# Sliding-window attention in 18 blocks with a DMA transpose of the output, instead of 17 blocks with a TensorE transpose

## The chip, the cores and the metric

The kernel runs on one NeuronCore of a Trainium2 chip. The core has TensorE (PE, matmuls), VectorE (DVE), ScalarE (ACT), GpSimd (POOL) and SyncE (SP), which here only issues DMAs. The metric is the device time of one execution in microseconds, lower is better. Several executions are timed, and one more is profiled.

## What is computed

A transformer layer with adaptive layer norm for 2048 tokens of 448 features. Attention has 16 heads of 28 features, and each token looks at 8 tokens: itself and every second one before it (dilation 2), so even tokens see only even tokens and odd ones only odd ones.

```python
mod = (silu(c) @ w_mod)                     # sa, ca, ga, sb, cb, gb
h = layernorm(x) * (1 + ca) + sa
qkv = h @ wqkv                              # 16 heads of 28
idx = pos[:, None] - (arange(8) * 2)[None, :]
logits = where(idx >= 0, q . k[idx] * 28 ** -0.5, -1e9)
o = softmax(logits) . v[idx]
x = x + ga * (o @ wo)
h = layernorm(x) * (1 + cb) + sb
x = x + gb * (gelu(layernorm(h) @ w1 + b1) @ w2 + b2)
```

## The kernel before

The tokens are stored as two halves: first the 1024 even ones, then the 1024 odd ones. In this order the window is the 8 nearest tokens of a half, and a block of queries needs a band of neighbouring keys. There are 16 stripes of 128 tokens.

**Front end.** For each group of stripes (0-1, 2-3, 4-7, 8-11, 12-15; the group's name is its first stripe) the input is normalized (`z`), transposed into feature-major form (`zt`: by TensorE for the first three groups, by DMA for the last two, L569), scaled (`h`, tile `hT`), and projected to keys and queries (`qk`, eight items a group, L599), which `qe` copies to `qT` and `kT`. These tiles have 16 columns of padding at both ends.

**Attention.** 17 blocks of 121 queries, each with 128 keys that begin 7 tokens before the first query (`attention`, L664). A block is a chain of items, and their names, followed by the block's number, are used throughout:
- `lt` (TensorE, L678): 16 matmuls, one a head, four at a time in row tiles of 32, give logits transposed (keys x queries) in four PSUM banks.
- `ex` (ScalarE, L689): four exponentials into the tile `et`, bfloat16.
- `mk` (VectorE, L696): `et` times a mask of zeros and ones that was expanded to all heads beforehand (`mask_rest`, L658); two blocks have small extra memsets, for the start of the sequence and the border of the halves.
- `pv` (TensorE, L711) and `ve`: the values of the 128 keys, straight from `hT`, and their copy to SBUF with a column of ones.
- `po` (TensorE, L721): weights times values for 16 heads; the column of ones gives the sum of the weights.
- `rd`, `on` (VectorE, L728 and L732): reciprocal of the sum, and the normalized output, tokens by 448 features.
- `pt` (TensorE, L742): four 128x128 transposes of `on` into PSUM. The last one starts at feature 320, so that no padding of `on` is needed; the output projection has zeros in the doubled rows.
- `ot` (ScalarE or VectorE, through `copy`): the transposed block goes to `oT`, which holds 1024 tokens, the second half over the first.

**Rest.** `wo` projects a stripe (L763), `x1` adds it to the input, and a second and third normalization (`s2`, `r2`, `z2`, `ml`, `ad`, `s3`, `r3`, `y`) give `y`, transposed by DMA (`yt`, L803) into `yT`. In chunks of four stripes the feed-forward part follows: `w1` and `wt` (L295 and L300), `ge` (ScalarE, L812), `w2` (L853), `fin` (VectorE, L866 and L868), and `out`, a store of the stripe (L872). The power in a normalization (`r2`, `r3`, `frs`) is computed by GpSimd (L469).

**Order.** All items are declared to a planner (`Plan`) with an estimated cost for each engine that may run them, what they need, and which buffers they take. `order()` sorts them by these costs and by constants (`PRI` for each kind, `NUDGE` for single items, `LOOK`, `PHASES` for how many attention blocks come before each chunk), picks the engine where there is a choice, and gives out the eight PSUM banks. The instructions are then issued in this order, so each engine, and SP with its DMAs, works through a fixed list and waits where an operand isn't ready. SP issues the loads, the transposes by DMA and the stores.

Of the kernel before, what the change touches and what calls it, by code (L numbers as in the profile page):

```python
# [17 lines left out]
KOFF_N = [0, 128, 256, 320]  # L18
ZR_N = 64
# [3 lines left out]
PADF = 16  # L23
BQ, BK = 121, 128
NBK = -(-S // BQ)
WT = PADF + S + PADF
# [5 lines left out]
PHASES = [9, 14, 17, 17]  # L32
# [11 lines left out]
LOOK = 0.000444  # L44

PRI = {"ad": -96.0, "agfst": 196.2, "ags2": 257.8, "ags3": 51.1, "ex": -118.3, "ge": -9.0, "h": 492.2,
       "lt": 26.7, "mk": -63.3, "ml": 15.5, "mod": -71.9, "on": -63.1, "ot": -130.2, "pb": -18.2, "po": 77.9,
       "ps": 105.4, "pt": 35.7, "pv": 19.9, "qe": -91.5, "qk": -123.7, "r3": 22.0, "rd": -24.1, "s2": -207.6,
       "s3": 72.9, "ve": -158.2, "w1": -18.3, "w2": -62.8, "wo": -144.0, "wt": 10.8, "x1": 20.5, "y": -37.1,
       "yt": -87.3, "z": 139.3, "z2": 81.0, "zt": -267.4}  # L50

NUDGE = {"ad10": -20.7, "ad6": -81.4, "ad8": 11.5, "ags2_0": 10.6, "ags2_11": -6.6, "ags2_14": -75.9,
       "ags2_2": -100.4, "ags2_5": -6.3, "ags2_8": -10.9, "ags3_11": -15.8, "ags3_14": 104.5, "ags3_3": 36.6,
       "ags3_5": -16.0, "ags3_7": -64.8, "ex11.2": 12.3, "fin9": -40.2, "frs12a": 19.8, "frs8a": 22.6,
       "ge2.10": 13.7, "ge2.8": 76.9, "ge3.12": 31.1, "h12.0": 37.1, "h4.2": 55.2, "h8.2": 78.5, "lt0": 93.2,
       "lt10": 29.5, "lt12": 5.8, "lt13": 52.0, "lt15": -33.2, "lt2": -20.6, "lt4": 58.9, "lt8": -8.9,
       "mk5": 34.4, "mk8": 47.0, "ml10": -42.6, "ml4": 10.8, "on12": -18.4, "on4": 8.5, "ot11": 74.0,
       "ot12": 9.8, "ot16": 53.8, "ot4": 60.9, "ot5": 22.7, "ot6": 65.9, "out13": -24.4, "out14": -59.4,
       "out8": -106.6, "pb_cbe": -184.9, "pb_gb": -36.7, "pb_gbe": -13.6, "po0": 8.9, "po1": -60.3, "po12": 10.8,
       "po15": -157.0, "pt10": 41.4, "pt12": 14.3, "pt5": -52.4, "pt8": -37.2, "pv1": -38.0, "pv13": -62.4,  # L60
       "pv4": 11.4, "pv7": 25.6, "qe12.0": -27.8, "qe12.3": 18.7, "qe12.5": 61.8, "qe2.0": -34.0, "qe2.1": 132.4,
       "qe2.2": 4.0, "qe2.3": 19.6, "qe2.4": 7.9, "qe2.6": 9.4, "qe2.7": -33.6, "qe4.0": 62.7, "qe4.7": -12.7,
       "qe8.0": 5.1, "qe8.1": -64.2, "qe8.7": -80.1, "qk0.1": 133.8, "qk12.0": 113.6, "qk12.6": 61.1,
       "qk4.1": -47.9, "qk4.3": 67.4, "qk4.4": 55.2, "qk4.5": -100.0, "qk4.7": 76.7, "qk8.7": -37.3,
       "r2_0": -89.0, "r2_0a": 57.1, "r2_10": 15.5, "r2_4": -9.3, "r2_6": -40.7, "r2_8": -62.2, "r3_0": 23.2,
       "r3_0a": 24.8, "r3_10a": -7.1, "r3_12": -88.9, "r3_12a": -80.6, "r3_6": 21.3, "r3_6a": -73.9, "r3_8": 9.0,
       "r3_8a": 38.0, "rd12": 24.6, "rd13": 26.1, "rd4": 14.1, "rd6": 54.8, "s2_11": 64.8, "s2_15": -82.0,
       "s2_5": -15.7, "s2_6": 35.8, "s2_8": 10.9, "s3_0": -51.5, "s3_1": 12.8, "s3_10": 26.8, "s3_11": 17.0,
       "s3_12": 28.7, "s3_13": -42.2, "s3_7": 38.2, "s3_9": -24.9, "w1_0.5": 32.1, "w1_1.6": 54.9, "w1_2.0": 6.1,
       "w1_2.2": -19.8, "w1_3.6": 57.3, "w2_11.1": 53.2, "w2_14.2": 103.0, "w2_14.3": 80.6, "w2_14.6": -16.7,  # L70
       "w2_15.2": -35.7, "w2_4.3": -44.4, "w2_5.6": 48.3, "w2_8.2": 135.9, "w2_9.2": 147.8, "w2_9.3": -21.2,
       "w2_9.4": -70.7, "w2_9.5": 107.8, "w2s2": 74.7, "wo0": 8.8, "wo1": 19.3, "wo11": -16.1, "wo8": 34.2,
       "wt_0.5": -16.3, "wt_2.3": -8.1, "wt_2.5": 20.1, "x1_1": 21.7, "x1_10": -25.3, "x1_11": -5.0,
       "x1_5": 27.9, "y11": -18.1, "y5": 40.1, "yt1": 28.5, "yt10": -133.2, "yt11": -10.4, "yt12": -68.4,
       "yt2": 6.1, "z1": 95.3, "z2": 138.5, "z2_10": 23.2, "z2_11": -10.3, "z2_12": -125.8, "z2_13": 16.8,
       "z2_2": 8.2, "z2_4": 21.3, "z2_5": 19.0, "z2_8": 41.6, "z2_9": 13.3, "z4": 6.2, "z8": 12.9, "zt13": -4.0,
       "zt4": 5.5, "zt8": 84.8}
# [162 lines left out]
def kernel(  # L240
# [65 lines left out]
    def ps_of(nm, n=512):  # L306
        return psum[P.bank[nm]][:, 0:n]

    hT = cst.tile([128, KT, WT], BF16, name="hT")
    qT = cst.tile([128, 4, WT], BF16, name="qT")  # L310
    kT = cst.tile([128, 4, WT], BF16, name="kT")
# [20 lines left out]
    mask1 = cst.tile([128, BK], BF16, name="mask1")  # L332
    mask_rest = cst.tile([128, H, BK], BF16, name="mask_rest")
# [4 lines left out]
    ybufs = [cst.tile([128, DP], BF16, name=f"ybuf{i}") for i in range(NYB)]  # L338
    NVB = 3
# [27 lines left out]
    load_ktiles(nc.sync, wo_s, A_wo, ZR_N)  # L367
# [22 lines left out]
    nc.vector.memset(wo_s[0:ZR_N, KT - 1, :], 0.0)  # L390
# [9 lines left out]
    pad_ranges = [(0, PADF), (PADF + S, WT)]  # L400
    for (a, b) in pad_ranges:
        nc.gpsimd.memset(hT[:, :, a:b], 0.0)
        nc.gpsimd.memset(kT[:, :, a:b], 0.0)
        nc.gpsimd.memset(qT[:, :, a:b], 0.0)
    nc.gpsimd.memset(mask1[:], 1.0)
    nc.gpsimd.affine_select(out=mask1[:], in_=mask1[:], pattern=[[1, BK]], compare_op=ALU.is_ge,
                            fill=0.0, base=WIN - 1, channel_multiplier=-1)
    nc.gpsimd.affine_select(out=mask1[:], in_=mask1[:], pattern=[[-1, BK]], compare_op=ALU.is_ge,
                            fill=0.0, base=0, channel_multiplier=1)

    def tok_col(b):
        return PADF + b * 128

# [197 lines left out]
    zs, h_of, fe_of = {}, {}, {}  # L611
# [39 lines left out]
    def b1_fn(e):  # L651
# [6 lines left out]
    P.add("mask", {"DVE": 0.65}, needs=["later"], fn=lambda e: nc.vector.tensor_copy(  # L658
        out=mask_rest[:], in_=mask1[:].unsqueeze(1).to_broadcast([128, H, BK])))

# [3 lines left out]
    def attention(g, exp_after, lt_after):  # L664
        q0 = PADF + g * BQ
        k0 = q0 - (WIN - 1)
        nq = min(BQ, S - g * BQ)
        fes = sorted({fe_of[min(max(t, 0), S - 1) // 128] for t in range(g * BQ - WIN + 1, g * BQ + BK)})
        fek = sorted({fe_of[min(max(t, 0), S - 1) // 128] for t in range(g * BQ - WIN + 1, g * BQ + BQ)})
# [4 lines left out]
        def l_fn(e):  # L674
            lts = T["lt", g] = [ps_of(f"lt{g}.{r}") for r in range(4)]
            for ft in range(4):
                for r in range(4):
                    nc.tensor.matmul(lts[r][:, ft * BK:(ft + 1) * BK],  # L678
                                     lhsT=kT[32 * r:32 * r + DH, ft, k0:k0 + BK],
                                     rhs=qT[32 * r:32 * r + DH, ft, q0:q0 + BK],  # L680
                                     start=True, stop=True, tile_position=(32 * r, 0))
        P.add(f"lt{g}", {"PE": 0.25}, rows=32, after=lt_after, needs=[f"qe{f}.{m}" for f in fes for m in range(8)], lag=0.17,
              allocs=[f"lt{g}.{r}" for r in range(4)] + [f"et{g}"], fn=l_fn)
        for r in range(4):
            def x_fn(e, r=r):
                if r == 0:
                    T["et", g] = wk.tile([128, H, BK], BF16, name="et", tag="et")
                et_v = T["et", g][:].rearrange("p (ft r) c -> p r ft c", r=4)
                nc.scalar.activation(out=et_v[:, r], in_=T["lt", g][r].rearrange("p (ft c) -> p ft c", ft=4),  # L689
                                     func=ACT.Exp, scale=float(DH) ** -0.5)  # L690
            P.add(f"ex{g}.{r}", {"ACT": 0.57}, needs=[f"lt{g}"], tab="exp",
                  after=exp_after + ([f"ex{g}.{r - 1}"] if r else []), uses=[f"lt{g}.{r}", f"et{g}"], fn=x_fn)

        def m_fn(e):
            et = T["et", g]
            nc.vector.tensor_tensor(out=et[:], in0=et[:], in1=mask_rest[:], op=ALU.mult)  # L696
            if g == 0:
                nc.vector.memset(et[0:WIN - 1, :, 0:WIN], 0.0)
            jx = SL - g * BQ
            if 0 < jx < BQ:  # L700

                px = jx + WIN - 1
                p0 = (px - (WIN - 1)) // 32 * 32
                assert px - 1 <= p0 + 31
                nc.vector.memset(et[p0:px, :, jx:jx + WIN], 0.0)
        P.add(f"mk{g}", {"DVE": 1.14}, needs=[f"ex{g}.{r}" for r in range(4)] + ["mask"], uses=[f"et{g}"], fn=m_fn)
# [11 lines left out]
        def o_fn(e):  # L718
            po = T["po", g] = ps_of(f"po{g}", H * (DH + 1)).rearrange("p (h d) -> p h d", h=H)
            for h in range(H):  # L720
                nc.tensor.matmul(po[:, h, :], lhsT=T["et", g][:, h, :], rhs=vbufs[g % NVB][:, h, :],  # L721
                                 start=True, stop=True)
# [212 lines left out]
```

## Time and profile before

| | |
|---|---|
| median of 3 runs | 182.32 us (181.95 to 182.45) |
| profiled execution | 182.19 us |
| its span, first to last instruction | 180.5 us |
| granted TensorE clock | 1.0 |
| HBM read, written | 9.41 MB, 1.84 MB |
| DMA traffic after the loads (from about 29 us) | short bursts: transposes and stores |

In rows of grouped instructions the columns are: line, engine, operation, output and inputs by the program's names, shapes and count; then the total busy time in microseconds and the mean duration of one in nanoseconds; then the engine's idle time before them and what ended it. `PEld` is TensorE's weight load, which overlaps its matmuls. In the chain that ended last, a row has a start, a length and what ran. A row of the waits names who waited, for whom, the total, the number of times and the longest. In the rows of DMA issues the last number is the median time from issue to landing.

### The profile page before, as it was taken

The numbers are of one execution on the slowest core, as the hardware profiler recorded it, in microseconds if no ns is written. First come the engines' busy times: TensorE is split into PE (matmuls) and PEld (weight loads), VectorE is DVE, ScalarE is ACT, GpSimd is POOL, SyncE is SP. The second block draws the span as 40 slices with busy tenths as digits, with TensorE's granted clock in tenths as the row PEclk, the third lists the DMA queues.
The fourth block names the chain that finished last, engine by engine and source line by source line (L and its number), as shares of the span: only waits on it lengthen the run. The fifth ranks groups of instructions, "written<-read, shape, count | busy, mean of one in ns | idle before, by whom it ended". The sixth has DMA issues, their size and how long they took to land.

```text
span 180.5 us, 3837 instructions
## 1 busy us (share of the span) xinstructions
PE 174.4 (97%) x1464; PEld 88.4 (49%) x1464; DVE 138.4 (77%) x348; ACT 118.6 (66%) x217; POOL 32.7 (18%) x67
## 2 busy tenths in 40 slices
PE   6989999999999999999999999999999999999992
PEld 2457566555555544444655454445643454433451
DVE  5789899799998999997989988688879865020251
ACT  2298996999898946999578475995835810077400
POOL 8413005000106403121403041100013400000000
PEclk9999999999999999999999999999999999999999
DMA  5999995441000530011051012031000025100011
GB/s 166 322 368 315 401 390 162 94 86 29 0 4 0 61 61 0 0 35 32 22 79 35 4 21 63 0 73 41 0 4 25 0 56 120 47 25 0 0 51 51
DMA packets 23376, 14.63 MB, mean 81 GB/s; under 512 B 13693, under 2 KB 22398, under 8 KB 23358
## 3 DMA queue, kind: packets, MB, share of 16 engines
q1 hardware_dynamic: 22334, 13.53, 27.0%
q10 hardware_dynamic: 1024, 0.86, 1.5%
q8 instruction: 11, 0.18, 0.4%
q14 instruction: 7, 0.06, 0.1%
HBM read 9.41 MB, written 1.84 MB: 62 GB/s over the span
## 4 chain that ended last, share of the span: by engine, by line
PE 72%; DVE 12%; DMA 4%; ACT 4%; SPq 2%; issue 2%; ACTq 1%; POOL 1%; DVEq 0%
PE ps L295 21%; PE ps L853 20%; PE ps L599 8%; PE ps L763 6%; PE ps L711 5%; PE ps L300 4%; DVE st L446 4%; DMA hT<-zbuf 3%; PE ps L721 3%; PE ps L678 2%; DVE et L696 2%; PE ps L742 2%; SPq L803 2%; DVE hT L589 2%; DMA yT<-ybuf 1%
## 5 line engine op out<-in xcount | busy, mean ns | idle before, releaser
L812 ACT ACTIVATE hm<-ps,b_col 128x512 bf16<-128x512 f32 x56 | 34.1, 692 | 23.2 <-PE ps L300 23.1
L853 PE MATMUL ps<-w_s,hm 128*128 128x448 bf16 x224 | 47.2, 353 | 0.0
L469 POOL TENSOR_TENSOR rs<-tv,neg_half 128x2 f32<-128x2 f32 (+1 forms) x21 | 20.4, 973 | 108.8 <-DVE ng L465 108.7
L295 PE MATMUL ps<-yT,w_s 128*128 128x512 bf16 x168 | 39.5, 380 | 0.5 <-DMA yT<-ybuf 0.5
L689 ACT ACTIVATE et<-ps 128x512 bf16<-128x512 f32 x68 | 36.1, 613 | 3.3 <-PE ps L678 3.0
L599 PE MATMUL ps<-hT,Wqk 128*128 128x512 bf16 (+1 forms) x160 | 31.3, 337 | 0.9 <-ACT Wqk L436 0.9
L853 PEld LDWEIGHTS <-hm 128*128 128x128 bf16 x224 | 21.0, 98 | 19.3 <-issue 0.9
L295 PEld LDWEIGHTS <-w_s 128*128 128x128 bf16 x168 | 15.5, 98 | 21.9 <-issue 5.3
L866 DVE TENSOR_TENSOR xt<-ps,gbb_bc 128x448 f32<-128x448 f32 x11 | 6.9, 624 | 22.3 <-PE ps L853 22.3
L696 DVE TENSOR_TENSOR et<-et,mask_rest 128x2048 bf16<-128x2048 bf16 x17 | 20.5, 1208 | 0.1
L599 PEld LDWEIGHTS <-Wqk 128*128 128x128 bf16 x160 | 14.6, 97 | 11.4 <-POOL nb L471 1.1
L446 DVE BATCH_NORM_STATS2 st<-x_all 128x6 f32<-128x448 bf16 x32 | 18.5, 613 | 0.1
L711 PE MATMUL ps<-Wv,hT 128*128 128x448 bf16 x68 | 15.7, 353 | 0.0
L763 PE MATMUL ps<-wo_s,oT 128*128 128x448 bf16 x64 | 14.1, 352 | 0.0
L768 DVE TENSOR_TENSOR x_all<-ps,x_all 128x448 bf16<-128x448 f32 x16 | 9.7, 619 | 3.1 <-PE ps L763 3.0
L436 ACT CAST vbuf<-ps 128x448 bf16<-128x448 f32 x14 | 7.6, 546 | 5.0 <-PE ps L711 5.0
L436 ACT CAST qT<-ps 128x512 bf16<-128x512 f32 (+1 forms) x19 | 9.6, 518 | 2.0 <-PE ps L599 1.5
L721 PEld LDWEIGHTS <-et 128*128 128x128 bf16 x272 | 9.0, 96 | 3.8 <-DVE et L696 0.9
L732 DVE TENSOR_TENSOR on<-ps,rden 128x448 bf16<-128x448 f32 x17 | 10.5, 616 | 0.2
L436 ACT CAST kT<-ps 128x512 bf16<-128x512 f32 (+1 forms) x18 | 8.9, 512 | 1.3 <-PE ps L599 1.1
L721 PE MATMUL ps<-vbuf,et 128*128 128x29 bf16 x272 | 9.5, 176 | 0.1
L446 DVE BATCH_NORM_STATS2 st<-z 128x6 f32<-128x448 bf16 x16 | 9.4, 612 | 0.1
(98 smaller groups left out, 188.7 us busy)
## 6 DMA issues: line engine op xcount, KB each, us to landing
w_s<-in_B_w_dram SPq DMA_DIRECT2D x2, 896.0 KB, 11.4
out_dram<-x_all SPq DMA_DIRECT2D x16, 112.0 KB, 1.7
w_s<-in_B_w_dram SPq DMA_DIRECT2D x1, 1568.0 KB, 13.7
wmod<-in_w_mod_dram SPq DMA_DIRECT2D x1, 1344.0 KB, 7.5
x_all<-in_A_x_dram SPq DMA_DIRECT2D x1, 896.0 KB, 10.4
wqk_st<-in_A_wqkv_dram SPq DMA_DIRECT2D x2, 336.0 KB, 5.8
x_all<-in_A_x_dram ACTq DMA_DIRECT2D x2, 224.0 KB, 4.2
x_all<-in_A_x_dram SPq DMA_DIRECT2D x1, 448.0 KB, 5.0
```

The costliest lines, as they stand in the source:

```text
L295: nc.tensor.matmul(o, lhsT=lhs(w, slice(0, 128), kt), rhs=rhs(slice(0, 128), kt), start=(i == 0), stop=False)
L436: nc.scalar.copy(out=out, in_=in_)
L446: nc.vector.bn_stats(out=st[:], in_=src())
L469: nc.gpsimd.tensor_tensor(out=rs[:], in0=T["tv", tile_key][:], in1=neg_half[:, 0:n], op=ALU.pow)
L599: nc.tensor.matmul(pq, lhsT=Wqk[:, kt, m, :], rhs=hT[:, kt, c0:c0 + w], start=(kt == 0), stop=(kt == KT - 1))
L689: nc.scalar.activation(out=et_v[:, r], in_=T["lt", g][r].rearrange("p (ft c) -> p ft c", ft=4), func=ACT.Exp, scale=float(DH) ** -0.5)
L696: nc.vector.tensor_tensor(out=et[:], in0=et[:], in1=mask_rest[:], op=ALU.mult)
L711: nc.tensor.matmul(pv, lhsT=hT[:, kt, k0:k0 + BK], rhs=Wv[:, kt, :], start=(kt == 0), stop=(kt == KT - 1))
L721: nc.tensor.matmul(po[:, h, :], lhsT=T["et", g][:, h, :], rhs=vbufs[g % NVB][:, h, :], start=True, stop=True)
L763: nc.tensor.matmul(pw, lhsT=oT[:, kt, jb * 128:(jb + 1) * 128], rhs=wo_s[:, kt, :], start=(kt == 0), stop=(kt == KT - 1))
L812: nc.scalar.activation(out=T["hm", c][:, ft, 0:w], in_=ps_of(f"p1_{c}.{ft}", w), func=ACT.Gelu_apprx_tanh, bias=b1_col[:, ft:ft + 1])
L853: nc.tensor.matmul(T["p2", b], lhsT=T["hm", c][:, ft, bi * 128:(bi + 1) * 128], rhs=w2_s[:, ft, :], start=(ft == 0 and b not in XPE), stop ...
```

## The change

Attention works in blocks that begin at multiples of 112 after a first block of 128 in each half: `BLOCKS` lists nine a half, 18 in all. A block of 112 queries has 128 keys, the first 16 of them before its first query; a block of 128 has exactly its own tokens as keys. So no block crosses the border of the halves, the padding of `hT`, `qT` and `kT` goes, and so do the two special memsets. There are two masks of one head's size, and the product broadcasts them over the heads. `et` has fixed buffers whose last 16 columns are set to one once, since `po` still works on 128 columns. `on` has fixed buffers of 512 features, the last 64 zero, and is transposed by one DMA from SP straight into `oT`: `pt`, its PSUM bank and the copy go, and the zero rows of the output projection move to its end.

```diff
-BQ, BK = 121, 128
-NBK = -(-S // BQ)
+BK = 128
+BLOCKS = [(p * SL + t, n) for p in range(2) for t, n in [(0, BK)] + [(BK + 112 * i, 112) for i in range(8)]]
+NBK = len(BLOCKS)
+BACK = BK - 112
...
-PHASES = [9, 14, 17, 17]
+PHASES = [10, 16, 18, 18]
...
-    pad_ranges = [(0, PADF), (PADF + S, WT)]
-    for (a, b) in pad_ranges:
-        nc.gpsimd.memset(hT[:, :, a:b], 0.0)
-        nc.gpsimd.memset(kT[:, :, a:b], 0.0)
-        nc.gpsimd.memset(qT[:, :, a:b], 0.0)
...
+    for m, back in zip(masks, (0, BACK)):
+        nc.gpsimd.memset(m[:], 1.0)
...
+    for et in ets:
+        nc.gpsimd.memset(et[:, :, BK - BACK:BK], 1.0)
+    for on in ons:
+        nc.gpsimd.memset(on[:, D:DP], 0.0)
...
-    P.add("mask", {"DVE": 0.65}, needs=["later"], fn=lambda e: nc.vector.tensor_copy(
-        out=mask_rest[:], in_=mask1[:].unsqueeze(1).to_broadcast([128, H, BK])))
...
-        q0 = PADF + g * BQ
-        k0 = q0 - (WIN - 1)
-        nq = min(BQ, S - g * BQ)
+        q0, nq = BLOCKS[g]
+        k0 = q0 if nq == BK else q0 - BACK
...
-                                     rhs=qT[32 * r:32 * r + DH, ft, q0:q0 + BK],
+                                     rhs=qT[32 * r:32 * r + DH, ft, q0:q0 + nq],
...
-            nc.vector.tensor_tensor(out=et[:], in0=et[:], in1=mask_rest[:], op=ALU.mult)
+            nc.vector.tensor_tensor(out=et, in0=et, in1=masks[nq < BK][:, 0:nq].unsqueeze(1).to_broadcast([128, H, nq]),
+                                    op=ALU.mult)
...
-            for kt in range(KT):
-                nc.tensor.transpose(out=pt[:, kt, :], in_=T["on", g][:, KOFF_N[kt]:KOFF_N[kt] + 128],
-                                    identity=ident[:])
-        P.add(f"pt{g}", {"PE": 0.2}, needs=[f"on{g}"], uses=[f"on{g}"], allocs=[f"pt{g}"], lag=0.2, fn=p_fn)
...
-                copy(e, oT[:, :, c0:c0 + n], T["pt", g][:, :, t:t + n])
...
-        P.add(f"ot{g}", {"ACT": 0.45, "DVE": 0.31}, needs=[f"pt{g}"] + old, uses=[f"pt{g}"], fn=c_fn)
+        P.add(f"ot{g}", {"SP": 1.25}, needs=[f"on{g}"] + old, uses=[f"on{g}"], lag=1.2,
+              fn=lambda e: nc.sync.dma_start_transpose(out=oT[:, :, c0:c0 + nq], in_=on_of[g][0:nq, :]))
```

The constants `PRI`, `NUDGE` and `LOOK` are other ones, so the order of nearly all items differs, also that of items that the change doesn't otherwise touch. On SP the first transposes stand as ot0, zt8, zt9, ot1, zt10, zt11, ot2, zt12 to zt15, ot3, ot4; before they were zt8 to zt15. On TensorE, `wo0` and `wo1` stand ahead of all `qk8`, and between `wo15` and the last chunk's `w1` (`w1_3.0`) stand 30 items of `w2`, one of `w1` and two of `wt`, where there were 34, four and three.

## The prediction

> **What bounds the kernel now.** I read the page's busy shares first, then the chain that ended last in order of time, then the waits, and only then the durations. The busy shares and the granted clock:
>
> ```profile
> PE 174.4 (97%) x1464; PEld 88.4 (49%) x1464; DVE 138.4 (77%) x348; ACT 118.6 (66%) x217; POOL 32.7 (18%) x67
> PEclk9999999999999999999999999999999999999999
> ```
>
> TensorE is busy for 97% of the span at full clock. Busy alone could hide gaps, since matmuls overlap, so the chain decides. From the first full projection matmul at 11.76 us on, TensorE never rests longer than a fraction of a microsecond, and between 45.75 and 146.54 us the chain is TensorE alone. Its rows give what one item costs from start to start (start us, length us, line):
>
> ```profile
> 45.75 0.57 PE ps L721 x16
> ...
> 46.32 0.87 PE ps L599 x4
> 47.19 0.22 PE ps L742 x4
> 47.42 0.34 PE ps L678 x16
> ...
> 51.22 0.40 PE ps L721 x16
> ...
> 64.74 0.76 PE ps L711 x4
> ```
>
> To be seen: four output transposes (`pt`, L742) 0.22, one block of logits (`lt`, L678) 0.34, weights times values (`po`, L721) 0.39 to 0.41 with the odd 0.57 that holds a wait, values (`pv`, L711) and output projection 0.76, one projection of 512 tokens 0.86 to 0.87. The waits of TensorE and its weight load:
>
> ```profile
> PE ps L295 <- DMA yT<-ybuf: 0.5, 1, 0.5
> ...
> PEld L721 <- DVE et L696: 0.9, 2, 0.5
> ...
> PEld L742 <- DVE on L732: 0.7, 3, 0.3
> ```
>
> Only the first is idle time of the array itself; the others are largely covered by matmuls still running. So work taken off TensorE shortens the time one for one, as long as nothing arrives later than its shorter queue asks for it. The end (last matmul 177.3, one DVE add, one store) is untouched.
>
> **TensorE, step by step.** 17 `pt` go: 17 x 0.223 (0.22 in the chain; starts in the timeline give 0.223) = -3.79. An eighteenth block comes: `lt` 0.34, and 0.10 because after every `lt` the next `pv` starts later (0.86 instead of 0.76 at 80.39), `pv` 0.76, `po` 0.41: +1.61. Net -2.18. Sixteen `lt` have 112 columns instead of 128. Their cost lies between unchanged (if issue sets it) and in proportion to the columns of four concurrent rows of tiles, 4 x 16 columns at the rate of the projection (512 columns in 0.216): -0.027 each, -0.43 in all. I take half, -0.2. The sum is -2.4, with ends -2.2 and -2.6.
>
> The row for `lt` is 16 matmuls in 0.34, 21 ns each. The Trainium skill (TensorE: Matmul & The Clock Gate, section "Wait — 56ns, not 53.3ns") says that starts never come closer than about 25 ns; 16 of those are 0.40, and by it the narrower blocks save nothing. The trace is already below that floor, so it does not close the question.
>
> **VectorE and ScalarE.** VectorE loses 9 of the 18 transposed-output copies (9 x 0.407 = 3.7), the mask expansion (0.69) and two memsets (0.2); it gains one `rd` and `on` (0.25 + 0.62). The mask product takes a broadcast mask on 1792 elements. Cheap end: 1.208 x 1792 / 2048 = 1.06; dear end, if the broadcast or the rows of 112 out of 128 cost the packed rate, the 2.01 of the product of 1792 elements with a float32 operand (L631). I take 1.06, since two products with a broadcast operand keep the rate:
>
> ```profile
> L696 DVE TENSOR_TENSOR et<-et,mask_rest 128x2048 bf16<-128x2048 bf16 x17 | 20.5, 1208 | 0.1
> ...
> L787 DVE TENSOR_TENSOR z<-z,g_bc 128x896 bf16<-128x896 bf16 x8 | 5.0, 623 | 0.2
> ...
> L648 DVE TENSOR_TENSOR w_s<-w_s,gb_bc 128x2240 bf16<-128x2240 bf16 (+1 forms) x3 | 3.7, 1239 | 0.0
> ```
>
> That is 16 x 1.06 + 2 x 1.21 = 19.4 against 20.5. VectorE: about -4.8 of 138. ScalarE loses 9 copies (9 x 0.524 = 4.7), pays 64 x 0.56 + 8 x 0.613 = 40.7 for exponentials instead of 41.7 (64 columns fewer are 0.053 by its casts, 0.595 at 512 and 0.385 at 256) and one more `ve` 0.55: about -5. Neither is counted: TensorE is what sets the time, so this only buys slack, most of it between 20 and 80 us where VectorE is 9 to 10 of 10 busy.
>
> **GpSimd.** Six pad memsets go (0.09 apart, 0.5); a second mask (0.86), two strips of `et` (256 elements, 0.3 each by 0.20 for 128 elements) and two of `on` (0.1 each) come: +1.1. They end at about 6.6 instead of 5.5, and the first power starts at 7.16 after 1.64 idle. Hidden by 0.5; uncovered, it would move everything by what exceeds that.
>
> **The DMA queue.** 18 transposes on SP join the 24 there:
>
> ```profile
> yT<-ybuf SPq DMA_TRANSPOSE x16, 2.5
> ...
> hT<-zbuf SPq DMA_TRANSPOSE x8, 2.5
> ```
>
> One holds SP for 1.21 (median; 1.19 to 1.92) and lands 2.4 to 4.4 after issue. No row has 112 partitions; the bounds are 7/8 of this and the slowest row, and I take the median. As a sum, 42 x 1.21 = 51 us between 27 and 150: no bound. The latency is: `on` to usable `oT` was 0.2 transpose, 0.2 for its end, 0.41 to 0.57 copy, about 1.0; it becomes 2.5. SP works in order, so an `ot` waiting for its `on` holds the transposes behind it. The built order shows where.
>
> *Early:* SP holds ot0, zt8, zt9, ot1, zt10, zt11, ot2, zt12 to zt15. `on0` stood at 31.47; the new order puts `pb_gae` (1.93), three statistics (1.65), the four `z` (0.94) and `mk1` (1.1) behind it and drops the mask copy (0.69), so it follows `po0`, which TensorE reaches at about 25: `on0` ends near 27. Six issues of 1.22 and 1.3 to land: zt11 is there at 35.8, `h8` (4 x 0.32 on VectorE) at 37.1. TensorE has ahead of `qk8` 5 `pv`, 5 `lt` (0.43), 3 `po`, 2 `wo`, 8 `zt`, 3 modulations, 16 projections of 256 tokens (0.436) and 8 of 512: 26.6 from 11.76, hence 38.4. Slack 1.3. `wo1` needs ot2, which lands near 37.0, and its turn is 37.6: slack 0.6.
>
> *Late:* from the end of `wo15` to `w1_3.0` TensorE has only 13.5 us of other work (it had 19.8: 133.0 to 153.4 less the wait). Ahead of it stand `x1_15` 0.58, statistics 0.6 + 0.2 + 0.25, power and product on GpSimd 1.2, `z2` 0.7, `ml` and `ad` 1.2, `fin11` 1.25, statistics 1.14 + 0.3 + 0.25, GpSimd 1.0, `y` 0.8 on ScalarE, while `fin7` and its store hold SP until 9.6; then two transposes, 1.2 and 2.5: 13.3. Slack 0.2, about what the old kernel had where it lost 0.5. The same sum for `wo11` to `w1_2.0` gives 13.3 against 13.7.
>
> So the four meeting points hold by 0.2 to 1.3 us. I add 0.3 for waits of a tenth or two there beyond those of the old kernel. **Forecast: -2.4 + 0.3 = -2.1.** The profiled execution took 182.19 (span 180.5, 1.7 around it), 0.13 under the median of the runs, 182.32; 182.19 - 2.1 = 180.1.
>
> **Rivals.**
>
> A, *the relief counts too*: the waits of the old kernel also go, 0.5 before `w1_3` and, by the starts of the matmuls in the timeline, about 0.6 in short waits elsewhere (0.2 each before two projections of `qk8` among them), with the whole 0.43 of the narrow `lt`: -2.6 - 1.1 = -3.7, 178.5. For it: VectorE and ScalarE each lose 5 us in the crowded part. Against: both meeting points of the feed-forward got tighter.
>
> B, *the handovers eat it*: `w1_2.0` and `w1_3.0` each come 1.0 late, because each of the twelve hops costs 0.07 to 0.1 more than my sums: -2.4 + 2.0 = -0.4, and with 0.1 to 0.3 elsewhere 182.0. For it: the old kernel waited at just this place. Against: there the feed-forward rows had stood behind two transposes and a store in the queue, and GpSimd took 1.6 once.
>
> C, *slower*: ot0 comes to SP while the weights still load. The first transpose of the old kernel, issued at 29.42, held SP for 1.92 and landed after 4.0, the later ones 1.2 and 2.5. If all six up to zt11 cost 1.92, `h8` ends 4.2 later than 37.1, 41.3 against 38.4: a wait of 2.9, and `mk3`, `x1_0` behind `h8` on VectorE follow it, so that another 1.0 is lost at `po3`. -2.4 + 3.9 = +1.5: 183.7. It decides from a mean of about 1.8 per transpose on. Against: DMA traffic ended at about 28.5 us in the old trace, so one or two are hit, not six.
>
> The Trainium skill (VectorE: DVE Perf Modes, section "The three transpose paths") gives 390 ns for a 128x128 square on TensorE and 1309 through DMA, and its table of rules says to use TensorE where PSUM will do. By it a four-square `ot` is an estimated 5.2 us and C the likely outcome. The trace has the four squares of `hT` and `yT` issued in 1.2 and landed in 2.5, so it does not bear that out.
>
> D, *the mask product does not keep its rate*: 18 x 0.95 = 17 us more on VectorE, half of it in the part where it has no room: at least +5, 187.
>
> **Numbers.** Forecast 0.62, A 0.12, B 0.09, C 0.14, D 0.03. 0.3% (0.55 us) is what a measurement of this kernel can tell. Faster: forecast and A nearly whole, 0.73; same: B and the forecast's edge, 0.10; slower: 0.17. The range goes from A's end, 178.5, to 183.0, half-way into C. The forecast's own range is 179.4 to 181.2.
>
> **What would show it.** No TensorE rows for the output transposes; `po`, `pv`, `lt` 18 times; the sum of TensorE's starts shorter by 2.2 to 2.6 between the first projection and the last matmul. `oT<-on` 18 times at SP with 1.2 each and 2.5 to land. The mask product at 1.06. TensorE waiting less than 1 us in all for `oT`, `hT` and `yT`. I am wrong if the waits of TensorE at `qk8`, `wo1`, `w1_2` or `w1_3` add to over 2 us, or if the mask product takes near 2 us.

## The result, and the profile after

The changed kernel takes 185.35 us (184.63 to 200.78, median of 4) beside 182.38 (181.95 to 182.45) of the kernel before: a ratio of 1.0155, 95% interval 1.012 to 1.019, slower by 1.5%. In the experiments it came to 184.66 beside 182.24, 1.015 (1.0104 to 1.0195). The prediction was -2.1 us; it is +2.4 to +3. The first profile of it fell in a disturbed execution (200.78 us, mean granted clock 0.85), so what follows reads another profiled execution of the same kernel: 184.45 us, span 182.7, granted clock 1.0.

The busy shares and the clock of the changed kernel:

```profile
PE 172.9 (95%) x1432; PEld 85.6 (47%) x1432; DVE 135.5 (74%) x338; ACT 115.3 (63%) x222; POOL 31.1 (17%) x68
PEclk9999999999999999999999999999999999999999
```

TensorE is busy for 1.5 us less (174.4 before), and so are VectorE and ScalarE, by 2.9 and 3.3; the span is 2.2 longer. So the time went into waits. TensorE's in the changed kernel, those that are new:

```profile
PE ps L293 <- DVE st L449: 1.5, 1, 1.5
PEld L738 <- DMA oT<-on: 0.8, 1, 0.8
PE ps L602 <- DVE qT L437: 0.7, 1, 0.7
PE ps L711 <- ACT hm L787: 0.7, 1, 0.7
```

To be seen: the longest is one wait of the first feed-forward matmuls (L293, `w1_0.0`), then `wo9` for its transposed output, a projection of the front end (`qk4.7`, which starts at 24.55), and one `po` (`po9`). The releaser in the first row is only the last event that the profile could find; the landing of the transposes decides, below.

The starts of all TensorE items, in the order in which they are issued, split the span at `w1_0.0`. "Work" is the sum over items of the shortest regular length of their kind (the durations of the prediction, and 0.307 for `lt` of 112 columns); what is left is waiting.

| us | before | after |
|---|---|---|
| first projection (`qk0.4`) starts | 10.32 | 11.85 |
| from it to `w1_0.0`: work, waits | 53.02, 3.10 | 51.29, 5.42 |
| `w1_0.0` starts | 66.44 | 68.56 |
| from it to the end of the last matmul: work, waits | 107.30, 3.55 | 106.23, 4.60 |
| last matmul ends | 177.29 | 179.39 |

TensorE's work fell by 1.73 and 1.07, 2.80 together. Its waits grew by 2.32 and 1.05, 3.37 together, and the first projection starts 1.53 later: -2.80 + 3.37 + 1.53 = +2.10, by which the last matmul ends later. (Of the 1.53 a part is only moved: the old kernel waited for 1.22 just behind its first projection, so its second one starts at 11.97 and the changed kernel's at 12.41.) The whole loss stands at one date: `w1_0.0` is 2.12 later although TensorE has 1.73 less to do until then. Behind it the 1.07 are given back, most of them in two waits, 0.82 before `po9` and 0.56 before `wo9`.

What `w1_0.0` needs are yt0 to yt3. SP's transposes in the timeline (start, length, engine's queue, line), of the kernel before and then of the changed one:

```profile
58.91 6.11 SPq L803 DMA_TRANSPOSE yT<-ybuf  x4
```

```profile
60.84 2.49 SPq L730 DMA_TRANSPOSE oT<-on  x2
63.42 3.24 SPq L778 DMA_TRANSPOSE yT<-ybuf  x2
```

Before, yt2 and yt3 were issued at 62.39 and 63.80, and the last landed at 66.31, just when TensorE came to it. After, `y2` is ready at 62.11, but ot5 and ot6 hold SP; yt2 and yt3 are issued at 63.42 and 64.73, the second holds SP for 1.93 instead of 1.2, and by the semaphores they land 4.30 and 3.62 after issue instead of 2.4: 68.35. So of the 2.0 that yT is later 0.9 is the place in the queue and 1.1 the landing. The DMA view of the changed kernel for 63 to 65.5 us (queue, kind: packets, MB, share of the 16 engines; then issues with the median time to landing) shows what else was there:

```profile
q1 hardware_dynamic: 983, 0.24, 82.6%
q8 instruction: 1, 0.02, 2.8%
...
yT<-ybuf SPq DMA_TRANSPOSE x2, 3.6
oT<-on SPq DMA_TRANSPOSE x1, 2.4
```

The queue `q8` carries one load of 16 KB of instructions (a code load, below). Experiments 9 to 11 move it by the number of TensorE's instructions, so it is TensorE's program. It runs from 64.64 to 65.77, while yt2 and yt3 are on their way.

### The profile page after: what moved, and what is told of

The parts are those of the page before. It is cut to its first block, busy times and chain, and to the rows that moved or that the text cites. A ratio compares the mean times of both kernels' runs of the same rounds, so it can differ in the third digit from the quotient of the medians.

```text
span 199.1 us, 3825 instructions
## 1 busy us (share of the span) xinstructions
PE 190.7 (96%) x1417; PEld 90.3 (45%) x1432; DVE 136.3 (68%) x338; ACT 116.7 (59%) x222; POOL 30.8 (15%) x68
## 4 chain that ended last, share of the span: by engine, by line
PE 90%; DVE 3%; POOL 2%; ACT 2%; issue 1%; POOLq 0%
PE ps L828 25%; PE ps L293 21%; PE ps L602 15%; PE ps L700 8%; PE ps L738 7%; PE ps L298 4%; PE ps L711 4%; PE ps L677 3%; PE ps L626 2%; ACT hT L589 1%; DVE st L449 1%; DVE hT L592 1%; DVE e_c L505 1%; PE ps L580 1%; PE ps L826 1%
## 5 line engine op out<-in xcount | busy, mean ns | idle before, releaser
L828 PE MATMUL ps<-w_s,hm 128*128 128x448 bf16 x224 | 52.7, 389 | 0.0
L293 PE MATMUL ps<-yT,w_s 128*128 128x512 bf16 x160 | 43.8, 419 | 0.8 <-PE ps L700 0.3
L686 ACT ACTIVATE et<-ps 128x448 bf16<-128x448 f32 (+1 forms) x72 | 35.5, 561 | 5.5 <-PE ps L677 5.2
L472 POOL TENSOR_TENSOR rs<-tv,neg_half 128x2 f32<-128x2 f32 (+1 forms) x21 | 17.9, 851 | 128.4 <-DVE ng L468 128.4
L602 PE MATMUL ps<-hT,Wqk 128*128 128x512 bf16 (+1 forms) x154 | 34.6, 367 | 1.0 <-DVE qT L437 0.5
L828 PEld LDWEIGHTS <-hm 128*128 128x128 bf16 x224 | 22.7, 105 | 23.7 <-issue 0.5
L293 PEld LDWEIGHTS <-w_s 128*128 128x128 bf16 x168 | 16.2, 103 | 26.0 <-issue 5.6
L693 DVE TENSOR_TENSOR et<-et,mask 128x1792 bf16<-128x1792 bf16 (+1 forms) x18 | 19.7, 1096 | 2.1 <-ACT et L686 2.1
L700 PE MATMUL ps<-Wv,hT 128*128 128x448 bf16 x72 | 18.0, 388 | 0.0
L738 PE MATMUL ps<-wo_s,oT 128*128 128x448 bf16 x64 | 16.2, 394 | 0.0
L700 PEld LDWEIGHTS <-hT 128*128 128x128 bf16 x72 | 7.0, 104 | 7.2
```

What stands on the lines that cost most here:

```text
L293: nc.tensor.matmul(o, lhsT=lhs(w, slice(0, 128), kt), rhs=rhs(slice(0, 128), kt), start=(i == 0), stop=False)
L472: nc.gpsimd.tensor_tensor(out=rs[:], in0=T["tv", tile_key][:], in1=neg_half[:, 0:n], op=ALU.pow)
L602: nc.tensor.matmul(pq, lhsT=Wqk[:, kt, m, :], rhs=hT[:, kt, c0:c0 + w], start=(kt == 0), stop=(kt == KT - 1))
L686: nc.scalar.activation(out=et_v[:, r], in_=T["lt", g][r][:, 0:4 * nq].rearrange("p (ft c) -> p ft c", ft=4), func=ACT.Exp, scale=float(DH) ...
L693: nc.vector.tensor_tensor(out=et, in0=et, in1=masks[nq < BK][:, 0:nq].unsqueeze(1).to_broadcast([128, H, nq]), op=ALU.mult)
L700: nc.tensor.matmul(pv, lhsT=hT[:, kt, k0:k0 + BK], rhs=Wv[:, kt, :], start=(kt == 0), stop=(kt == KT - 1))
```

## The experiments

Where an experiment leaves `oT` out, the output projection reads `hT`, which has the same shape.

**1. The changed kernel again**, and **2, 3. GpSimd's memsets at the head.** The first run is the one read above.

> The changed kernel again, for a profile at full TensorE clock. Both theories expect 184.6 to 185.4. Theory T (the meeting points and the head lose time): TensorE's starts hold about 2.2 to 2.6 less work than before, the head up to the first projection is 0.1 to 1.0 later, and waits of TensorE of 4 to 5 in all appear where oT, hT, yT or copies come late. Rival R (the items themselves got dearer): no new waits, but matmul items take longer from start to start than before.

The second puts the memsets of masks, `et` and `on` behind the long one of `wmod`; the third gives the kernel before five more memsets ahead of it.

```diff
-    for m, back in zip(masks, (0, BACK)):
...
     nc.gpsimd.memset(wmod...)
     (memsets of vbuf)
+    for m, back in zip(masks, (0, BACK)):
...
```

> The changed kernel with GpSimd's memsets of masks, et and on moved behind its long memset of the modulation weights. Theory P (VectorE's first small operation on e_c waits for the long GpSimd memset, which the new memsets push back by 1.0): e_c takes 0.4 or less instead of 1.4, the first power starts 0.9 to 1.3 earlier than in the changed kernel, and the time falls by 0.7 to 1.3, to about 184.2. Rival Q (the head is covered, the first projection waits for other copies): first power earlier, time within 0.3 of the changed kernel.

```diff
+    spare = [cst.tile([128, BK], BF16, name=f"spare{i}") for i in range(5)]
+    for sp in spare:
+        nc.gpsimd.memset(sp[:], 1.0)
```

> The kernel before with five extra GpSimd memsets of 128 columns (about 1.0 in all) put ahead of its masks, no other change. Theory P: e_c ends 1.0 later, the first power 1.0 later, and the time rises by 0.6 to 1.1, to 183.0 to 183.5. Rival Q: GpSimd had 1.6 of idle time before its first power, so the delay of 1.0 is hidden and the time rises by less than 0.3.

Measured: with the memsets late 184.26, 1.0129 (1.0066 to 1.0192), not told apart from the changed kernel; with five more in the kernel before 183.25, 1.0053 (1.0022 to 1.0084), +1.0 as expected. The place is an operation of VectorE on four elements, in the timelines of the kernel before (first two lines, with GpSimd's memset) and of the changed kernel:

```profile
4.80 0.38 DVE L502 TENSOR_SCALAR e_c<-e_c 128x4 f32<-128x4 f32 x1 [0.81 <-ACT e_c L524]
3.57 1.59 POOL L421 MEMSET wmod<- 64x1792 bf16 x1
```

```profile
4.79 1.42 DVE L505 TENSOR_SCALAR e_c<-e_c 128x4 f32<-128x4 f32 x1 [0.73 <-ACT e_c L527]
4.60 1.59 POOL L424 MEMSET wmod<- 64x1792 bf16 x1
```

It ends when the memset ends, at 5.16 and at 6.19; where the memset is over by then (experiment 2, 3.77) it takes 0.18. The Trainium skill (SBUF — State Buffer, section "SBUF: two separate sides") says that VectorE, in some of its operations, and GpSimd share a pair of ports as a lock held for a whole instruction; the trace agrees. So this operation ends 1.0 later in the changed kernel. But taking that back brought only 0.2 at `w1_0.0` (68.33 for 68.56): TensorE was 1.0 ahead up to `wo1` (38.36 for 39.36), and what came earlier then waited at `zt13`, which held SP for 2.47, and again for yT.

**4, 5. What the output transposes cost.** One run issues them all but lets nothing wait for their landing; the other issues none.

```diff
-                nc.tensor.matmul(pw, lhsT=oT[:, kt, jb * 128:(jb + 1) * 128], ...
+                nc.tensor.matmul(pw, lhsT=hT[:, kt, jb * 128:(jb + 1) * 128], ...
```

> The changed kernel, but the output projection reads hT in place of oT; all transposes of the output are still issued on SP, so their place in the queue stays and only the wait of TensorE for their landing goes. Theory L (the landing of the output transposes is what TensorE waits for): the waits before wo1 (0.25), wo9 (0.56) and part of the one before w1_0.0 go, -0.8 to -1.5 against the changed kernel, about 183.4. Theory Q (their place on SP ahead of the transposes of y is what costs): the 1.66 before w1_0.0 stays, so -0.5 to -0.8, about 184.0, and yt2 is still issued behind ot6. Theory O (neither; the order of the other items costs): -0.3 to 0.

```diff
-              fn=lambda e: nc.sync.dma_start_transpose(out=oT[:, :, c0:c0 + nq], in_=on_of[g][0:nq, :]))
+              fn=lambda e: None)
```

> The changed kernel without any transpose of the output: none is issued, and the output projection reads hT in place of oT. Theory Q: yt2 is issued at about 62.2, yt3 at 63.4, both landed by 66.0, the wait of 1.66 before w1_0.0 goes, and the wo9 and wo1 waits too: -2.0 to -2.6 against the changed kernel, about 182.3, and 1.2 or more under the kernel that issues them without landing. Theory L: within 0.5 of the kernel that issues them without landing. Theory O (the order of other items, not the output transposes, makes the waits): the waits at 23 us (0.84), before w1_0.0 (at least 0.8 left, since y2 and y3 come late) and before po9 (0.82) stay, and the time is -0.8 to -1.5, 183.2 or more.

Measured: 185.45, 1.0194 (1.0153 to 1.0235), and 183.03, 1.0049 (1.0031 to 1.0067). The landing costs nothing by itself: the wait before `wo9` goes, and `w1_0.0` is 0.55 later. Issuing them costs 2.4 by these two medians and 1.1 by the profiled executions; two of the four executions behind the first median have a mean clock of 0.99, which the last section takes up. But with no output transpose at all, on TensorE or on SP, the kernel is still slower than before, with 2.8 us less work on TensorE. Its chain of waits (start, length, what):

```profile
61.85 0.32 DVE ybuf L482
62.17 0.87 DVE et L692
63.04 4.43 DMA yT<-ybuf
67.47 0.14 issue
67.61 1.46 PE ps L293 x6
```

yt3 is issued at 63.04, as early as theory Q said, but lands only at 67.47: a code load from 65.35 on falls on its end. So the three theories were all too simple, and two questions came of it: does TensorE's work count at all ahead of `w1_0.0`, and what does a code load cost.

**6 to 9. Does TensorE's work count one for one?** The kernel before without output transposes (`pt` and its copies): all 17, the late ones (blocks 9 to 16), the early ones (0 to 7), and the early ones with TensorE's program kept at its old length.

```diff
-        ..., allocs=[f"pt{g}"], lag=0.2, fn=p_fn)
+        ..., allocs=[f"pt{g}"], lag=0.2, fn=(lambda e: None) if g < 8 else p_fn)
```

> The kernel before without its output transposes: no pt on TensorE, no copies to oT, and the output projection reads hT in place of oT; its order is otherwise the same. It is to the kernel before what the changed kernel without any output transpose is to the changed one. If TensorE's work counts one for one: 17 x 0.223 = 3.8 less, 178.5 to 179.0. Rival (pt filled time in which TensorE would have waited anyway): 1 to 2.5 less, 180 or more.

> The kernel before without the output transposes and copies of blocks 9 to 16, eight of the nine that stand behind w1_0.0; the projections of stripes 8 to 15 read hT in place of oT. Theory T (TensorE's work counts one for one only after the first w1, up to which the date of the first four yT decides): 8 x 0.223 = 1.8 less, or 1.3 to 1.8 with a short wait, 180.6 to 181.1. Rival (TensorE's work counts one for one nowhere, since the kernel before without any of them was no faster): 0 to 0.5 less.

> The kernel before without the output transposes and copies of blocks 0 to 7, the eight that stand ahead of w1_0.0; the projections of stripes 0 to 7 read hT in place of oT. Theory T: the 1.8 us that TensorE no longer works are waited for, most of them at lt5, qk12.2 and w1_0.0, which starts at 66.4 or, with a code load on yt2 or yt3, up to 2 us later: 182.0 to 184.0, no gain. Rival (TensorE's work counts one for one): 1.8 less, 180.5.

```diff
     def idle(n, out):
+        if n == NIDLE[0]:
+            for i in range(36):
+                nc.tensor.matmul(out[0:32, i:i + 1], lhsT=idle_in[:, 0:32], rhs=idle_in[:, 0:1], start=True, stop=True)
+            n = 6
```

> The kernel before without the output transposes and copies of blocks 0 to 7 (the projections of stripes 0 to 7 read hT in place of oT), and at the head two of eight idle warm-up matmuls replaced by 36 of a single column, which give TensorE's program back 68 instructions for the 64 that were left out, so that its code loads stand where they stood before. Theory F (the slowdown of the run without them is a code load on yt2 and yt3): the load comes at about 61.5, yt2 and yt3 land 2.5 after issue, w1_0.0 starts at 66.1 to 66.5 and the time is that of the kernel before, 181.9 to 182.6, since VectorE sets the date of yT. Rival (without the transposes something else delays yt2 and yt3): w1_0.0 at 68 and 184 or more, as without the shift. Second rival (TensorE's work does count there): 180.5 to 181.2.

| left out of the kernel before | median, ratio to before | `w1_0.0` starts | from there to the last matmul's end |
|---|---|---|---|
| nothing | 182.3 | 66.44 | 110.85 |
| all `pt` | 182.60, 1.0028 (1.0001 to 1.0054) | 68.63 | 109.2 |
| late `pt` | 180.83, 0.9919 (0.9893 to 0.9945) | 66.40 | 109.4 |
| early `pt` | 186.10, 1.016 (1.0095 to 1.0224) | 68.22 | 110.8 |
| early `pt`, program length kept | 183.04, 1.0045 (1.0027 to 1.0062) | 66.86 | 110.8 |

The late ones give 1.5 of their 1.8 us. The early ones, 1.8 us of TensorE's work taken away, give nothing. They cost some 1.7 in the two executions at full clock (183.96 and 184.19) and 3.8 by the median, since three of the five have a mean clock of 0.99. The chain of the kernel before, and that of the kernel without the early ones, at the same place:

```profile
65.50 0.22 PE ps L742 x4
65.72 0.76 PE ps L623 x4
66.48 1.64 PE ps L295 x7
```

```profile
63.71 0.15 DVE on L732
63.86 4.22 DMA yT<-ybuf
68.08 0.14 issue
68.22 1.89 PE ps L295 x8
```

Before, TensorE sets the date of `w1_0.0`, but only just: yT landed at 66.31. Without the early transposes TensorE is there hardly earlier, at 66.2: what it saved it has waited for at `po2` (0.5), `lt5` (0.6 for 0.24) and `qk12.2` (0.7 for 0.19). Then it waits for yT, which a code load from 63.84 on lets land 1.8 late. With 68 instructions put back at the head the load stands at 62.02, yt3 lands at 66.73, and what is left is no gain (+0.7). The head is not the reason: from the second projection, at 11.97, TensorE's starts are those of the kernel before for 20 us. But the first loads came earlier too, and one at 34.6 let `zt11` land 4.1 after its issue, so that VectorE's `h8` starts 1.3 later and y2 0.57 later. So this run is not free of a new hit either; without it `w1_0.0` would stand at about 66.3, an estimate from 66.86 and the 0.57.

What sets the date of yT is seen at `h12` on VectorE, here in the timelines of the kernel before and of the one without the early transposes:

```profile
41.92 1.06 DVE L589 TENSOR_SCALAR hT<-hT,ca_col,sa_col 128x512 bf16<-128x512 bf16 x3 [0.35 <-DMA hT<-zbuf]
```

```profile
42.10 1.06 DVE L589 TENSOR_SCALAR hT<-hT,ca_col,sa_col 128x512 bf16<-128x512 bf16 x3 [0.91 <-DMA hT<-zbuf]
```

In both it waits for `zt15`, which lands at 41.80 and 41.98, and from there to y2, at 62, nearly all of VectorE's items are later by the same 0.18. VectorE lost four copies in that run as well, 1.6 us, and that gave no earlier date either. So the chain ahead of `w1_0.0` runs from SP's transposes of the input over VectorE, with GpSimd and ScalarE in its last steps, to yT, and TensorE's work does not set its date. That VectorE has little room on the way is a row of the windows of the kernel before (stretch; busy us of each engine, with the number of instructions; clock, DMA share, GB/s):

```profile
40.00:66.00 26.00, 25.84 (x282) 13.75 (x280) 24.75 (x61) 22.67 (x45) 5.96 (x8) 1.00 0.17 26
```

VectorE, the third, is busy for 24.75 of 26 us.

**10, 11. Moving the code loads.** Both kernels with more single-column matmuls at the head (66, and one of the eight wide ones left).

```diff
     def idle(n, out):
+        if n == NIDLE[0]:
+            for i in range(66):
+                nc.tensor.matmul(out[0:32, i:i + 1], lhsT=idle_in[:, 0:32], rhs=idle_in[:, 0:1], start=True, stop=True)
+            n = 1
```

> The changed kernel with eight idle warm-up matmuls of TensorE at the head replaced by one of them and 66 of a single column: TensorE has 118 more instructions before its first real work, and nothing else differs. Theory F (each 16 KB load of TensorE's code that falls on a DMA transpose holds it and delays its landing, and where it falls is set by the count of TensorE's instructions): every load comes about 5.8 us earlier in TensorE's work, the one at 64.6 at about 59; yt3 lands 2.4 us after its issue instead of 3.6, the wait before w1_0.0 falls from 1.66 to 0.4 or less and the one before wo9 (0.56) goes: -1.2 to -1.9, about 183.3. A new hit on zt10 or zt11 near 35 us may take up to 1.0 of it at qk8. Rival (the long transposes come from the traffic or the place in the queue): the same transposes, zt13, yt3, yt5 and ot10, are held for 1.7 us or more, and the time is within 0.3.

> The kernel before with the same replacement of idle matmuls, so that its code loads come about 5.8 us earlier too. Theory F: the load at 155.0 comes at about 149, on yt13 and yt14, and w1_3.0 waits 1.3 to 2 instead of 0.6; others move off yt4 and onto free places: +0.4 to +1.4, about 183.2. Rival: the same transposes are long and the time is within 0.3 of the kernel before.

Measured: 186.64, 1.0237 (1.0201 to 1.0273), and 183.77, 1.0073 (1.0052 to 1.0094). Up to 65 us the loads came 4 to 6 us earlier, and other transposes were hit than before: in the changed kernel `zt13`, yt3, yt5 and ot10 are held for 1.19 to 1.26, and zt11, ot4 and yt8 for 1.7 to 2.4. That part of theory F held, and the gain did not: zt11's hold became a wait of 0.96 before `wo1`, one at 153.6 on yt15 a wait of 1.24 before `w1_3.0`, and yt3 still took 3.29 to land, with an 8 KB load on it at 67.16. In the kernel before a load on zt11 cost 1.56 near 35 us, and yt13 and yt14 were not hit, other than expected.

**12 to 16. Mending the order.** Each mend takes away a wait of the changed kernel that the trace shows.

```diff
     todo = P.order()
+    move("ot6", "yt3")
+    move("wo5", "w1_0.0")
```

> The changed kernel with ot6 moved on SP behind yt3, and on TensorE wo5, which needs ot6, moved behind w1_0.0. Theory Q: yt2 is issued at 62.2, yt3 at 63.4, w1_0.0 starts at 66.1 to 67.0 without a wait over 0.5, and the time falls by 1.0 to 1.6, about 183.3. Rival (y2 and y3 themselves, late by the stretched power on GpSimd, set it, or the next meeting point takes it back): w1_0.0 is earlier by less than 1, or later waits grow, and the time falls by less than 0.5.

Measured: 186.20, 1.0207 (1.0175 to 1.0238), slower. yt3 was issued at 63.83, 0.9 earlier, and a code load at 65.00 made its landing 3.86; ot6 behind it was held for 2.02, and `on7` waited for its buffer until ot6 had landed.

```diff
+    (the memsets late, as in experiment 2, and the two moves)
+    P.ops[P.index["h4.1"]]["ran"] = "DVE"
+    P.ops[P.index["h4.2"]]["ran"] = "ACT"
```

> The changed kernel with three mends of its order together: the memsets for the two masks, et and on behind the long one of wmod on GpSimd; ot6 behind yt3 and wo5 behind w1_0.0; and h4.1 on VectorE, h4.2 on ScalarE, so that no two engines take turns on one PSUM bank of the transposed input. Theory O (the change itself gains and what was lost is the order's): 0.9 at the head, 0.84 at 23 us and 1.0 to 1.6 before w1_0.0 are gained, -2.7 to -3.3, about 181.6, faster than before. Rival (each gain is taken back by the next fixed point, the transposes of stripes 12 to 15 on SP): not more than -1.5, 183 or slower.

Measured: 183.79, 1.0083 (1.0056 to 1.011). The wait of 0.84 at 23 us is gone, and 0.7 of the head's. `w1_0.0` starts at 66.50, the old kernel's date, but still after a wait of 1.52, again with a code load on yt3; the loss now stands behind it, where `wo5` was moved to and TensorE waits 0.55 before `wo5`, 1.14 before `po9` and 0.67 before `wo9`.

```diff
-    NON = SLOTS["on"]
+    NON = 3
...
+    P.ops[P.index["z2_6"]]["ran"] = "DVE"
     (and the 66 single-column matmuls of experiments 10 and 11)
```

> The changed kernel with the three mends of before (memsets late on GpSimd, yt2 and yt3 ahead of ot6 with wo5 behind w1_0.0, h4 by one engine per bank), and three more: a third buffer for on, so that on7 needn't wait until ot6 has landed; z2_6 on VectorE, so that ScalarE's GELU items needn't wait behind it for GpSimd; and the same shift of the code loads. Theory O+F: of the 5.9 us of waits of the mended kernel those before w1_0.0 (1.5), wo5 (0.55), po9 (1.1) and wo9 (0.7) fall to a quarter: 180.6 to 181.6, faster than the kernel before. Rival (what is won at one place is waited for at the next): 182.5 or more.

Measured: 184.16, 1.0102 (1.0067 to 1.0137). The waits before `po9` and `wo9` are gone and that before `w1_0.0` is 0.58; `qk0.4` starts at 12.33, and yt15 is hit: 1.69 before `w1_3.0`.

The next two keep these mends, without the 66 matmuls, and move `lt11`; the second of them puts 11 single-column matmuls at the head in the place of one wide one.

```diff
+    move("lt11", "w2_2.3")
```

> The changed kernel with the mends of its order and no shift of the code loads: memsets late on GpSimd; ot6 behind yt3, wo5 behind w1_0.0; h4 by one engine per PSUM bank; three buffers for on; z2_6 on VectorE; and lt11 behind w2_2.3, since it waits for a bank of w2_0. The first mended kernel lost 1.52 before w1_0.0, 0.55 before wo5, 1.14 before po9, 0.67 before wo9. Theory O+F: the code load at 63.6 still falls on yt3, so w1_0.0 still waits about 1.3; po9's and most of wo5's waits go: 1.3 less than the first mended kernel, 182.2 to 182.7, no different from the kernel before. Rival (what is won is waited for later): 183.3 or more.

```diff
+            for i in range(11):
...
+            n = 7
```

> The same, with one of the eight idle warm-up matmuls replaced by eleven of a single column: 20 more TensorE instructions, so that its code loads come some 1 us earlier. Theory F: the load at 63.6 comes at about 62.4, during yt2 instead of yt3, so that yt3 lands at about 65.3 instead of 66.3; w1_0.0 waits 0.2 to 0.5 instead of 1.3, w1_3.0 isn't hit (load at about 162): 0.8 to 1.1 less than the kernel without the shift, 181.2 to 181.8, faster than the kernel before. Rival (a hit on yt2 holds yt3 for as long): within 0.3 of the kernel without the shift.

Measured: 184.71, 1.0113 (1.0062 to 1.0165), and 183.78, 1.0059 (1.0029 to 1.009). The rival came true in both: TensorE comes to `w1_0.0` 2.6 and 1.9 us earlier than in the changed kernel and waits 2.24 and 1.89, with a code load on yt3 (4.75 and 4.39 to land). The 20 instructions did not move that load to other work: in both runs it begins during `po7`.

**17, 18.** The mended kernel without output transposes, and with a larger shift (66 single-column matmuls and four wide ones).

> The changed kernel with all the mends of its order (no shift of the code loads), without its output transposes: none is issued, and the output projection reads hT in place of oT. Theory O (two losses of about equal size, one of the order and one of the output transposes on SP): the mends take 1.7 to 2.5 off the 183.0 of the unmended kernel without output transposes, 180.6 to 181.3, so that the transposes cost the mended kernel 3 to 4. Rival (the mends won nothing, each gain waited for at w1_0.0 whatever stands on SP): 182.5 to 183.5.

> The changed kernel with all the mends of its order, and at the head four of eight idle matmuls replaced by 66 of a single column, so that the code loads come about 6 us earlier in TensorE's work and TensorE is busy until its first real work (with only one of eight left it rested for 1.25 us and its clock was low until 10 us). Theory F: no load falls on yt2 and yt3, w1_0.0 waits under 0.7; one falls on yt14 or yt15, w1_3.0 waits 1.2 to 1.7: 182.3 to 183.2, near the kernel before. Rival (w1_0.0 waits for something else): 184 or more.

Measured: 181.21, 0.9942 (0.9921 to 0.9963), and 187.27, 1.0289 (1.0236 to 1.0343). So the mends are worth 1.8 where no output transpose is on SP (183.03 to 181.21), and the transposes cost the mended kernel 3.5 (184.71 to 181.21; 2.4 by the profiled executions). Of the 3.5 a part is the clock: four of the five executions behind 184.71 have a mean of 0.99, and the fifth took 183.00. Even without any output transpose the mended order gains only 1.1 us, with 2.8 us less work on TensorE. The last run is a miss: `w1_0.0` waited 0.58 as expected, but the head was 0.5 later than in the changed kernel and two code loads at 91 us let ot9 land 4.15 after its issue, which became 2.2 before `wo8`, and the clock fell to 0.5. No kernel here that computes all of the output transposes, by the changed blocks, is faster than the one before.

## Why the prediction was wrong

**The work on TensorE: right.** -2.8 for -2.4. The narrow `lt` saved the whole 0.027 each (0.307 for 0.335), 19 ns a matmul. The Trainium skill (TensorE: Matmul & The Clock Gate, section "Wait — 56ns, not 53.3ns?") has a floor of about 25 ns; these row tiles are below it.

**"So work taken off TensorE shortens the time one for one": this step failed.** It holds behind `w1_0.0` (late `pt`: 1.5 of 1.8) and not ahead of it (early `pt`: nothing of 1.8). 1.73 of the 2.80 lie ahead. The condition that the prediction added, as long as nothing arrives later than asked, was tested at four meeting points, and the one with the least slack was not among them: in the old trace yT landed 0.13 before `w1_0.0` started. TensorE did not wait there, so no row of waits showed it; what would have is the landing of yt3, 66.31, beside the start at 66.44, and VectorE's 24.75 of 26 ahead of it.

**"+0.3 for waits": mis-sized, and at other places.** All waits together grew by 3.37. At `qk8`, `w1_2.0` and `w1_3.0` the changed kernel does not wait; at `wo1` 0.25. So the prediction's own sign of being wrong, over 2 us at these four places, did not appear. The waits at `w1_0.0` (1.66), `qk4.7` (0.84), `po9` (0.82) and `wo9` (0.56) were on no list. The first is the transposes' place on SP and a code load, 0.9 and 1.1 by the trace; no run takes away only one of the two without a new hit. The second is h4.2 on VectorE behind h4.3 on ScalarE, both reading one PSUM bank; giving each bank one engine took the wait away (experiment 13). The third is a GELU on ScalarE that stands behind `z2_6`, which waits for GpSimd, in the chain of the changed kernel:

```profile
82.80 0.89 POOL nb L474
83.69 0.03 issue
83.72 0.76 ACT z L480
84.47 0.58 ACT hm L787
85.06 0.04 issue
85.10 0.55 PE ps L711 x16
```

With `z2_6` on VectorE it was gone. None of these two comes from the DMA; they are the new order's.

**GpSimd, "hidden by 0.5": failed.** The cover was counted up to GpSimd's first power. What counted was VectorE's operation beside the long memset, which had no room: it ends 1.0 later. Alone in the kernel before this cost 1.0; in the changed kernel only 0.2 of it is left at `w1_0.0`.

**The DMA queue: right in size, wrong in place.** 1.19 to hold SP and 2.4 to land (medians), up to 3.9 with a code load, and no bound as a sum. The prediction followed the queue early and late, and not at 60 to 65, where ot5 and ot6 stand ahead of yt2.

**The mask product** kept its rate: 1.08 where 1.06 was forecast. **VectorE and ScalarE** lost 2.9 and 3.3 where 4.8 and 5 were forecast, and in 40 to 66 us VectorE is as full as before (24.71 of 26).

**The rivals.** Slower was right, with the wrong place: the six early transposes that were to take 1.92 took 1.20 to 1.29. The late handovers held, and the mask did not fail.

## What to carry to other kernels

Ask for each stretch which engines are full, not for the whole: an engine that is 97% busy gains nothing from less work in a stretch whose next hand-over is set by a chain through another engine that is 95% busy. A hand-over without a wait can still have no slack: compare the landing with the start, since 0.1 between them means that both arrive together. Before a transfer is put into a queue, look what stands behind it there and who waits for that; and price a memset by what waits beside it.

## What was not expected of the hardware

**Code loads delay DMA transposes.** In 19 profiles, from 50 us on, 260 transposes were in flight with no load of instructions: every one landed 2.33 to 2.50 us after issue and held SP for under 1.27. Of 115 with a 16 KB load in the same time 89 took over 2.7, up to 4.92, and 39 held SP for 1.4 to 2.72 instead of 1.2, as none of the 260 did. Of 59 with an 8 KB load alone 18 took over 2.7, up to 3.42. A load of 16 KB lasts 0.9 to 1.6. The Trainium skill (DMA: Bandwidth & Descriptors, section "Queues, rings and completion order") says that a DMA engine takes turns between queues by whole packets; a packet of 16 KB in front of transposes in packets of under 512 bytes fits that, but no run here shows the mechanism. Where loads fall depends on the number of TensorE's instructions: in all 19 profiles the fifth load of 16 KB, the one that falls on yt2 and yt3 in the changed kernel, begins after 1178 to 1224 of its matmuls and weight loads, whatever the kernel, and the loads follow each other after 246 on average. So leaving 64 out moved one by 2.4 us, onto yt2 and yt3, and putting them back moved `w1_0.0` from 68.22 to 66.86.

**A wait of 2 us can cost two more.** In the profiled execution of the mended kernel without a shift (184.19, its median 184.71) TensorE rested from 64.5 to 66.6. Its windows (stretch; PE busy; clock, DMA share, GB/s):

```profile
64.00:66.00 2.00, 0.51 (x3) 1.00 0.35 64
66.00:68.00 2.00, 1.21 (x3) 0.60 0.32 59
68.00:70.00 2.00, 2.00 (x7) 0.55 0.00 0
70.00:72.00 2.00, 2.00 (x25) 1.00 0.00 0
```

The clock is 0.55 to 0.60 up to 70, and the first matmuls of `w1_0.0` start 0.43 apart instead of 0.22. In the trace it is 0.5 for one stretch of 3.4 us, from 66.4 to 69.8; the run of experiment 18 has the same stretch from 93.4 on, after a rest of 2.06 us. One such stretch makes the mean of an execution 0.99, and executions with 0.99 are some 2 us longer than others of the same kernel. A rest of this length does not always end so: in experiment 4 TensorE rested for 2.17 before `w1_0.0` and the clock stayed at 1.0, while two other executions of that kernel have 0.99. The changed kernel's wait of 1.66 had no such end in its profile. The Trainium skill (TensorE: Matmul & The Clock Gate, section "What's actually happening") has the clock halved after an idle window of about 3.4 us; here it was halved after rests of 2.1, and what decides between two rests of that length no run here shows.

**Single-column matmuls did not warm TensorE.** In experiment 18, after 66 of them and four wide ones, the next wide ones start 0.43 apart; in the changed kernel, where eight wide ones fill the same time, the next ones start 0.22 apart. The row of the clock shows 1.0 in both.
